# Strassen's scheme in the second layer of the second sweep too, in seven PSUM banks, with the tokens held once

## The chip, the cores and the metric

The kernel runs on one core of a Trainium2 chip. The metric is the time of one execution on the device, in microseconds (us); the median of three executions is given. Engines are TensorE (PE in the profile; PEld is its weight load), VectorE (DVE), ScalarE (ACT), GpSimd (POOL) and SyncE (SP), which issues the DMA transfers.

## The reference

Attention with a decay, then a mixing of the tokens and a two-layer perceptron with a residual. B = 8, H = 8, S = 576, D = 64, so d_model is 512; the hidden width is 2048, the rank of U V is 32. All is float32.

```python
def _attn_ref(q, k, v, f):
    scores = scale * np.matmul(q, k.transpose(0, 1, 3, 2))
    cum = np.cumsum(np.log(np.clip(f, 0.0001, 1.0)), axis=-1)
    scores = np.where(causal, -1000000000.0, scores + cum[:, :, :, None] - cum[:, :, None, :])
    ...                                   # softmax over the last axis
    return np.matmul(attn, v)

def _moe_ref(x, U, V, w_ch1, w_ch2):      # x: 8 x 576 x 512
    h = x.transpose(0, 2, 1) @ U @ V
    u = x + h.transpose(0, 2, 1)
    return u + np.maximum(u @ w_ch1, 0.0) @ w_ch2
```

## The kernel before

Every float32 operand of a product is held as a high and a low part in the matmul's own format, and a product is three matmuls: high by high, low by high, high by low. `split` makes the two parts: a cast on ACT (L182) and a subtraction on DVE or POOL (L185).

The hidden layer has 16 chunks of 128. A first sweep computes the attention batch by batch, the mixing, u, and the part of the perceptron of the first 6 chunks, and leaves u (`ud`, both parts) and the running output (`accd`) in DRAM. The second sweep, which the change touches, does the other NB = 10 chunks, whose weights (b1h, b1l, b2h, b2l) DVE and ACT decode into SBUF in its first part (L65 to L71). Tokens are worked on in nine groups of 512: the first 512 of each batch, and one group of the eight last 64.

Group 0 is plain: `first` (L979) and the plain second layer. Groups 1 to 8 take the chunks in five pairs (`pair_of_chunks`). The first layer of a pair is a product of 2 x 2 blocks by the scheme of Strassen and Winograd: seven products (m1 to m7) of six matmuls of 256 columns (`product`, L1069), each in one of two psF or two psX banks. DVE adds them up from PSUM (L1092; the copy of m1 to s1 is ACT's, L1100), and ACT and DVE make the relu and its split (L970, L971). The second layer (`second`, L993) is plain: per pair eight units of three matmuls of 512 columns, which add up over the ten chunks in four psO banks. `go` issues three, three and two of the units of the pair before between the products of a pair.

The scheme needs sums of blocks of the weights (`weight_sums`, DVE and ACT, made once at the start) and of the tokens. For these, POOL makes eight sums per group (`token_sums`, L1052 to L1057) in `whole_u`, which lies in xn[2], and in the last pair of a group, when each part has been read for the last time, `token_part` splits it into Th (ACT) and Tl (POOL). A group's u comes by two transfers of 1 MB (`load_u`, L962) into one of two buffers, its running output by one (L1138), and its four outputs are stored at the end (L999) after DVE's last adds (L997).

PE's order is the program's; the other engines' queues are ordered by a scheduler from a model of the kernel. On the chip each queue runs in the order it was given, and an instruction waits for semaphores. Waits on PSUM are by bank.

Of the kernel before, what the change touches and what calls it, by code (L numbers as in the profile page):

```python
# [40 lines left out]
def tile_decay_attention_moe(ctx, tc, qk, v, f, U, V, w1, w2, out):  # L41
# [917 lines left out]
    def load_u(g):  # L959
        t = up.tile([P, 2, NDC, MAIN], F32R, tag="u", name=f"u{g}")  # L960
        for x in range(2):
            nc.sync.dma_start(t.bitcast(F32)[:, x], ud[g, :, x])  # L962
# [22 lines left out]
    def second(z, i, h, x):

        k = z["done"][x]
        z["done"][x] += 1
        if k == 0:
            z["po"][x] = psO.tile([P, DM], F32, tag="O", name=f"O{z['g']}_{x}")  # L990
        po = z["po"][x]
        for m, (ht, wt_) in enumerate(((h[0], b2h), (h[1], b2h), (h[0], b2l))):
            nc.tensor.matmul(po, ht[:, P * x : P * x + P], wt_[i], start=k == 0 and m == 0, stop=k == NB - 1 and m == 2)  # L993
        if k < NB - 1:
            return
        g, o = z["g"], z["acc"][:, x]
        nc.vector.tensor_tensor(o, po, o, op=ALU.add)  # L997
        if g < B:
            nc.sync.dma_start(out[g, P * x : P * x + P], o)  # L999
# [9 lines left out]
    for i in range(NB // 2):  # L1009
# [35 lines left out]
    whole_u = xn[2][:, 0:4].rearrange("p q (c t) -> p q c t", c=2)  # L1045

    def token_sums(u):

        for q in range(4):
            c, t = 2 * (q // 2), HT * (q % 2)  # L1050
            h, l = (x[:, c : c + 2, t : t + HT].bitcast(F32) for x in u)
            nc.gpsimd.tensor_tensor(whole_u[:, q], h, l, op=ALU.add)  # L1052
# [6 lines left out]
    def token_part(q):  # L1059
        split(Th[:, q], Tl[:, q], whole_u[:, q], nc.scalar, nc.gpsimd)  # L1060
# [3 lines left out]
    def product(bank, tag, name, a, b):  # L1064
        ps = bank.tile([P, 512], F32, tag=tag, name=name)[:, 0:HT]
# [7 lines left out]
    def pair_of_chunks(z, u, i, ready, renew):  # L1073

        def go(k):
            for fn in ready[:k]:
                fn()
            del ready[:k]  # L1080
# [130 lines left out]
```

## Time and profile before

| | us |
|---|---|
| three executions | 1246.3, 1245.42, 1245.12; median 1245.42 |
| profiled execution | 1242.59, span 1240.8, granted TensorE clock 0.999 |
| PE, PEld busy | 1204.0, 1066.0 |
| DVE, ACT, POOL busy | 861.3, 645.5, 424.5 |
| second sweep, group 0 | about 753 to 806 |
| groups 1 to 8 | 806 to 1237; 52.8 a group from the second on (u loads at 860.43, 913.25, 966.08) |

In rows of a timeline stand: start, duration, engine, line, operation, output and input tiles with their shapes, how many, and in brackets the idle time of the engine before and what ended it. The chain's rows have start, duration, engine, tile, line and count. `SPq` is a DMA that SP issues.

### The profile page before, as it was taken

Reading aid. Unit: us, or ns where it says so; the run is one execution under the profiler, and the core shown is the slowest. Engines: PE = TensorE matmul, PEld = TensorE weight load, DVE = VectorE, ACT = ScalarE, POOL = GpSimd, SP = SyncE. Lnnn points to the kernel's source line nnn. Section 1 sums busy time; section 2 is a strip of 40 time slices with the busy share of each in tenths; the row PEclk is TensorE's granted clock in tenths of the full one; section 3 lists DMA queues with packets and bytes.
Section 4 is the critical chain, followed back from the end, with each engine's and each line's share of the span. In section 5 each row is a group of like instructions: output and inputs, shape, how many; then the busy total and the mean of one; then the engine's idle time right before and its main releaser. Section 6 shows DMA issues by size and latency. Waiting matters only on the chain.

```text
span 1240.8 us, 21851 instructions
## 1 busy us (share of the span) xinstructions
PE 1204.0 (97%) x7824; PEld 1066.0 (86%) x7824; DVE 861.3 (69%) x2195; ACT 645.5 (52%) x1741; POOL 424.5 (34%) x377
## 2 busy tenths in 40 slices
PE   8998999999999999999999999989999999999998
PEld 5776898998989988989989888878988889888897
DVE  8877778768778778787686799684554645546443
ACT  5777678767778758777675444322122221212211
POOL 4223454534544435454541000441341413315100
PEclk9999999999999999999999999999999999999999
DMA  6544344525335325425342345121120312213010
GB/s 183 153 132 130 79 105 111 151 68 159 95 89 164 88 78 148 117 71 171 79 125 76 120 141 229 34 69 69 68 102 35 136 43 95 85 52 137 1 35 35
DMA packets 67581, 125.87 MB, mean 101 GB/s; under 512 B 7408, under 2 KB 31984, under 8 KB 65424
## 3 DMA queue, kind: packets, MB, share of 16 engines
q1 hardware_dynamic: 67408, 124.47, 32.8%
q8 instruction: 62, 1.02, 0.3%
q14 instruction: 47, 0.39, 0.1%
q10 hardware_dynamic: 64, 0.00, 0.0%
HBM read 88.65 MB, written 35.78 MB: 100 GB/s over the span
## 4 chain that ended last, share of the span: by engine, by line
PE 82%; DVE 8%; ACT 6%; issue 2%; DMA 2%; SPq 0%; ACTq 0%; POOL 0%; DVEq 0%; POOLq 0%
PE O L993 20%; PE M L1069 16%; PE A L700 10%; PE B L718 9%; PE V L543 5%; PE T L440 3%; PE S L344 3%; PE Hb L979 2%; PE V L515 2%; PE S L345 2%; ACT P L373 1%; ACT G L309 1%; PE Tt L609 1%; PE St L344 1%; PE S L341 1%
## 5 line engine op out<-in xcount | busy, mean ns | idle before, releaser
L1092 DVE TENSOR_TENSOR sum<-M,sum 128x256 f32<-128x256 f32 x280 | 117.7, 422 | 173.3 <-PE M L1069 172.3
L970 ACT ACTIVATE bh<-sum 128x256 fp32r<-128x256 f32 x160 | 66.3, 418 | 256.9 <-DVE sum L1092 256.8
L373 ACT ACTIVATE P<-S,nm 128x128 f32<-128x128 f32 (+3 forms) x256 | 137.5, 539 | 57.5 <-DVE nm L365 48.3
L365 DVE CUSTOM_DVE_ANT_0 S<-S,mask 128x128 f32<-128x128 f32 (+3 forms) x256 | 125.7, 495 | 53.5 <-PE S L345 46.8
L993 PE MATMUL O<-b2h,bh 128*128 128x512 f32 x360 | 143.0, 397 | 0.0
L993 PE MATMUL O<-b2l,bh 128*128 128x512 f32 x360 | 142.4, 396 | 0.0
L993 PE MATMUL O<-b2h,bl 128*128 128x512 f32 x360 | 141.8, 394 | 0.0
L700 PE MATMUL A<-uh,w1h 128*128 128x256 f32 (+1 forms) x384 | 120.3, 313 | 1.8 <-DVE hl L704 1.7
L309 POOL CAST G<-qk 64x576 fp32r<-64x576 f32 x52 | 34.9, 671 | 250.1 <-PE St L345 149.5
L700 PE MATMUL A<-ul,w1h 128*128 128x256 f32 (+1 forms) x384 | 113.5, 296 | 0.0
L700 PE MATMUL A<-uh,w1l 128*128 128x256 f32 (+1 forms) x384 | 113.5, 296 | 0.0
L185 POOL TENSOR_TENSOR Tl<-xn,Th 128x512 fp32r<-128x512 f32 x32 | 41.3, 1303 | 201.7 <-PE M L1069 178.1
L971 DVE SCALAR_TENSOR_TENSOR bl<-sum,bh 128x256 fp32r<-128x256 f32 x160 | 92.4, 581 | 19.4 <-ACT bh L970 19.0
L1052 POOL TENSOR_TENSOR xn<-u 128x512 f32<-128x512 f32 x32 | 43.7, 1391 | 167.6 <-DVE b1l L71 106.4
L718 PE MATMUL B<-w2h,hh 128*128 128x512 f32 x216 | 90.4, 418 | 2.3 <-DVE hl L704 1.3
L440 PE MATMUL T<-ident,P 128*128 128x128 f32 x544 | 85.5, 273 | 0.0
L718 PE MATMUL B<-w2l,hh 128*128 128x512 f32 x216 | 85.1, 394 | 0.0
L718 PE MATMUL B<-w2h,hl 128*128 128x512 f32 x216 | 84.6, 392 | 0.0
L422 DVE TENSOR_TENSOR PTl<-T,PTh 128x512 fp32r<-128x512 f32 (+1 forms) x156 | 79.0, 524 | 6.6 <-ACT PTh L419 6.3
L993 PEld LDWEIGHTS O<-b2l,bh 128*128 128x128 f32 x360 | 67.7, 188 | 16.5
L322 POOL TENSOR_TENSOR G<-qk,G 64x576 fp32r<-64x576 f32 x52 | 74.4, 1431 | 15.6 <-ACT G L309 6.2
L993 PEld LDWEIGHTS O<-b2h,bl 128*128 128x128 f32 x360 | 68.2, 189 | 11.2
(240 smaller groups left out, 3543.7 us busy)
## 6 DMA issues: line engine op xcount, KB each, us to landing
qk<-in_qk_dram SPq DMA_DIRECT2D x104, 288.0 KB
u<-ud SPq DMA_DIRECT2D x16, 1024.0 KB
sr<-in_w_dram SPq DMA_DIRECT2D x20, 512.0 KB
vr<-in_v_dram SPq DMA_DIRECT2D x32, 256.0 KB
accd<-ost SPq DMA_DIRECT2D x32, 256.0 KB
xn<-accd SPq DMA_DIRECT2D x8, 1024.0 KB
out_dram<-xn SPq DMA_DIRECT2D x32, 256.0 KB
ud<-uh SPq DMA_DIRECT2D x7, 1024.0 KB
```

The lines of the kernel that those rows point to most:

```text
L322: pin(el.tensor_tensor(g[oth, 2, cols], k[oth], gf[oth, 2, cols], op=ALU.subtract))
L365: nc.vector.tensor_tensor_reduce(ps[:, :w], ps[:, :w], mask[:, 512 - w : 512], scale=-SCALE, scalar=3.0e38, op0=ALU.add, op1=ALU.min, accu ...
L373: nc.scalar.activation(pt, ps[:, :w], AF.Exp, bias=z["nm"][:, col : col + 1], scale=-1.0, accum_out=z["sm"][:, col : col + 1])
L422: defer(2, lambda: nc.vector.tensor_tensor(dstl, src, dsth.bitcast(F32), op=ALU.subtract))
L440: nc.tensor.transpose(tp[:, P * x : P * x + P], z["P"][j][i][:, P * c : P * c + P], ident)
L700: nc.tensor.matmul(ps[:, :nt], wt[:, fc, c], ut[:, c, sl], start=m == 0, stop=m == 3 * NDC - 1)
L718: nc.tensor.matmul(ps, ht[:, fc, P * x : P * x + P], wt[:, fc], start=fc == 0 and m == 0, stop=fc == NA - 1 and m == 2,)
L970: nc.scalar.activation(hh, src, AF.Relu)
L971: nc.vector.scalar_tensor_tensor(hl, src, 0.0, hh.bitcast(F32), op0=ALU.max, op1=ALU.subtract)
L993: nc.tensor.matmul(po, ht[:, P * x : P * x + P], wt_[i], start=k == 0 and m == 0, stop=k == NB - 1 and m == 2)
L1069: nc.tensor.matmul(ps, a[x][:, c], b[y][:, c], start=m == 0, stop=m == 5)
L1092: nc.vector.tensor_tensor(dst, ps, other, op=ALU.add)
```

## The change

The second layer of groups 1 to 8 goes by the same scheme. The hidden blocks X11, X12, X22 and four sums of them (S3, S1, S2, S4) lie in one buffer `hb`. After a pair's m3, DVE makes the four sums from relus with four instructions (L1218 to L1221), and ACT and POOL split them (L185). `output_products` then gives seven units of 2 x 3 matmuls of 256 columns (L1130), which add up over the five pairs of a group in seven banks, five of psM and two of psF. One such unit stands after each first-layer product. At the end of a group, in pair 0 of the next, the seven banks are combined into the four quadrants of the output: eight adds on DVE, a copy to u4 on ACT and three adds on POOL (all in `ends`, by `add`, L1112); only then are the quadrants stored.

All first-layer products use the two halves of one bank, `halves`. Tokens are held once: three blocks that enter a product as they are come into `direct` (six transfers of 256 KB, L969, in the last pair of the group before), and `load_whole` (L973) brings the high parts into xn[2] and the low ones into xn[0], from which POOL makes the token sums in place (L1086 to L1091). `acc` has one home, xn[1] (load L1265).

`weight_sums2` makes the sums of blocks of w2 on POOL and ACT: twelve POOL instructions of 128x256 for each of five pairs, four pairs in group 0 and the last in group 1.

```diff
-    up = pool("up", 2)
-    hp_ = pool("hp", 4)
-    psO = ctx.enter_context(tc.tile_pool(name="psO", bufs=4, space=PSUM, reuse_waits="tile"))
-    psX = ctx.enter_context(tc.tile_pool(name="psX", bufs=2, space=PSUM, reuse_waits="tile"))
+    psM = ctx.enter_context(tc.tile_pool(name="psM", bufs=1, space=PSUM, reuse_waits="tile"))
+    psL = ctx.enter_context(tc.tile_pool(name="psL", bufs=1, space=PSUM, reuse_waits="tile"))
+    direct = two.tile([P, 3, 2, 2, HT], F32R, name="direct")
+    hb = two.tile([P, 7, 2, HT], F32R, name="hb")
+    def load_direct(g, k):
+        c, t = ((0, 0), (2, 0), (2, HT))[k]
         for x in range(2):
+            nc.sync.dma_start(direct.bitcast(F32)[:, k, x], ud[g, :, x, c : c + 2, t : t + HT])
+    def load_whole(g):
+        for x, home in enumerate((xn[2], xn[0])):
+            nc.sync.dma_start(home[:, 0:NM], ud[g, :, x])
...
+    wides = [sf2.tile([P, 2 * HT], F32, tag="ost", name=f"sum{x}") for x in range(2)]
+    ends = sf.tile([P, 2 * HT], F32, tag="TS", name="sum2")
+    tmp = [t[:, HT * y : HT * y + HT] for t in [ends] + [x[:, NM] for x in xn] for y in range(2)]
+    def weight_sums2(i):
+        eng = nc.gpsimd
+        def whole(dst, r, c):
+            h, l = block2(i, r, c)
+            eng.tensor_tensor(dst, h.bitcast(F32), l.bitcast(F32), op=ALU.add)
...
+        for src, (h, l) in zip((t1, t0, t2, t3), [block2(i, 0, 1)] + SD[i]):
+            split(h, l, src, nc.scalar, eng)
+    halves = psL.tile([P, 2, HT], F32, name="halves")
+    def product(a, b):
+        ps = halves[:, turn[0] % 2]
+        turn[0] += 1
...
+    def output_products(z, i):
+        def ends_1():
+            nc.scalar.copy(u4, z["M"][1])
+            add(quarter[0], z["M"][1], quarter[0])
+        def ends_6():
+            add(u4, z["M"][6], u4)
+            add(u3, z["M"][7], u4)
+            add(u4, z["M"][5], u4)
+            for q in (2, 3):
+                add(quarter[q], u3, quarter[q], nc.gpsimd)
...
+        def ends_3():
+            add(quarter[1], z["M"][3], quarter[1])
+            add(quarter[1], u4, quarter[1], nc.gpsimd)
...
+        work = (
+            (1, X11, block2(i, 0, 0)), (4, X22, sd[2]), (2, X12, block2(i, 1, 0)), (7, S3, sd[0]),
+            (5, S1, block2(i, 0, 1)), (6, S2, sd[1]), (3, S4, block2(i, 1, 1)),
+        )
...
+        m1 = pr(1, block(i, 0, 0), D1)
         nc.scalar.copy(s1, m1)
+        slot(1)
+        m6 = pr(6, W2, T2)
+        add(s2, m6, s1)
+        slot(6)
+        m5 = pr(5, W1, T1)
+        add(s4, m5, s2)
+        slot(5)
+        m2 = pr(2, block(i, 0, 1), D2)
+        add(c11, m2, s1)
+        relu(*X11, c11)
+        slot(2)
+        m7 = pr(7, W3, T3)
+        add(c22, m7, s4)
+        add(s2, m7, s2)
+        relu(*X22, c22)
+        slot(7)
+        m4 = pr(4, block(i, 1, 1), T4)
+        add(c21, m4, s2)
+        relu(*X12, c21)
+        slot(4)
+        m3 = pr(3, W4, D3)
+        add(c12, m3, s4)
+        slot(3)
+        nc.scalar.activation(r21, c12, AF.Relu)
+        nc.vector.scalar_tensor_tensor(c22, c22, 0.0, r21, op0=ALU.max, op1=ALU.add)
+        nc.vector.scalar_tensor_tensor(r21, c11, 0.0, r21, op0=ALU.max, op1=ALU.subtract)
+        nc.vector.scalar_tensor_tensor(c11, c11, 0.0, c22, op0=ALU.max, op1=ALU.subtract)
+        nc.vector.scalar_tensor_tensor(c21, c21, 0.0, c11, op0=ALU.max, op1=ALU.add)
+        for src, (h, l) in ((r21, S3), (c22, S1), (c11, S2), (c21, S4)):
+            split(h, l, src, nc.scalar, nc.gpsimd)
+        ready.extend(output_products(z, i))
...
+                def renew(k):
+                    if k in (1, 2, 3):
+                        load_direct(nxt, k - 1)
+                    else:
+                        token_part({6: 3, 5: 0, 7: 1, 4: 2}[k])
+                pair_of_chunks(z, i, ready, renew if nxt is not None and i == NK - 1 else None, 1 if n > 1 or i else 2)
...
+                if i == 1:
+                    nc.sync.dma_start(xn[1][:, 0:NM], accd[g].rearrange("x p d -> p x d"))
+                    if nxt is not None:
+                        load_whole(nxt)
+                if i == 2 and nxt is not None:
+                    token_sums()
```

**How it moves instructions.** First PE, inside a pair. Before (m3, then the last two units of the second layer, then the next pair's first product; M are first-layer products, O second-layer sums, sw block sums of weights):

```order
L1069 MATMUL M_6_2_13911<-u_13136,swhh 128x256 [waits DVE_49]
L1069 MATMUL M_6_2_13911<-u_13136,swhl 128x256
...
L993 MATMUL O_2_13775<-b2h_9166,bh_2_13739 128x512
L993 MATMUL O_2_13775<-b2h_9166,bl_2_13740 128x512
L993 MATMUL O_2_13775<-b2l_9176,bh_2_13739 128x512
L993 MATMUL O_3_13800<-b2h_9166,bh_2_13739 128x512
...
L1069 MATMUL M_6_3_13933<-u_13136,b1h_9150 128x256 [waits DVE_49]
```

And after (from the unit of S2 past m5's follower to m2 and m7; halves is the one bank of the first layer, N the banks of the second):

```order
L1130 MATMUL N_8_13974<-b2h_9173,hb 128x256 x2
L1130 MATMUL N_8_13974<-b2l_9183,hb 128x256
...
L1107 MATMUL halves<-direct,b1h_9144 128x256 [waits DMAHW7_49,DVE_49]
L1107 MATMUL halves<-direct,b1l_9154 128x256
...
L1130 MATMUL N_8_13990<-sw_9772,hb 128x256 [waits Activation_49]
L1130 MATMUL N_8_13990<-sw_9772,hb 128x256 [waits Pool_49]
L1130 MATMUL N_8_13990<-sw_9772,hb 128x256 x4
L1107 MATMUL halves<-Th,swhh 128x256 [waits DVE_49]
```

Units of the second layer and products now alternate one by one; every product waits for the reader of the one before it, since both lie in one bank, and the units of S sums wait for POOL's splits.

Second POOL, from the end of one of the groups to the second pair of the next. Before:

```order
L1055 TENSOR_TENSOR xn_107<-xn_107 128x512
L1056 TENSOR_TENSOR xn_107<-xn_107 128x512
L1057 TENSOR_TENSOR xn_107<-xn_107 128x512
L185 TENSOR_TENSOR Tl<-xn_107,Th 128x512 x4
L1052 TENSOR_TENSOR xn_107<-u_13136 128x512 x4
```

After (xn_107 is xn[2], xn_105 is xn[0], xn_106 is xn[1] with `acc`; sum_9780 and sum_9781 are u3 and u4; hb rows are the splits, in the order S3, S1, S2, S4):

```order
L185 TENSOR_TENSOR Tl<-xn_107,Th 128x512 x3
...
L1086 TENSOR_TENSOR xn_107<-xn_107,xn_105 128x2x256 x4
L1088 TENSOR_TENSOR xn_107<-xn_107 128x2x256
L1089 TENSOR_TENSOR xn_107<-xn_107 128x2x256
L1090 TENSOR_TENSOR xn_107<-xn_107 128x2x256
L1112 TENSOR_TENSOR xn_106<-sum_9780,xn_106 128x2x256 x2
L1091 TENSOR_TENSOR xn_107<-xn_107 128x2x256
L185 TENSOR_TENSOR hb<-xn_106,hb 128x256
L1112 TENSOR_TENSOR xn_106<-sum_9781,xn_106 128x2x256
L185 TENSOR_TENSOR hb<-xn_106,hb 128x256
L185 TENSOR_TENSOR hb<-xn_105,hb 128x256
```

Between the Tl rows and the sums stand the four splits of pair 4, left out here; the three hb rows at the end are S3, S1 and S2 of the new group's pair 0, so they stand behind seven and eight token sums.

Third DVE, in pair 1 of a group. Before (the sums s2, s4, c11 and s3 of pair 1, then a relu's split; sum tiles are the temporaries):

```order
L1092 TENSOR_TENSOR sum_9780<-M_6_1_13751,sum_9780 128x256 [waits PE_49,Activation_49]
L1092 TENSOR_TENSOR sum_9781<-M_6_1_13759,sum_9780 128x256 [waits DVE_49,PE_49]
L1092 TENSOR_TENSOR sum_9782<-M_6_1_13779,sum_9780 128x256 [waits PE_49]
L1092 TENSOR_TENSOR sum_9781<-M_6_1_13787,sum_9780 128x256 [waits PE_49]
L971 SCALAR_TENSOR_TENSOR bl_2_13740<-sum_9782,bh_2_13739 128x256 [waits Activation_49]
```

After (the third row is c11 = m2 + s1 of pair 1):

```order
L1221 SCALAR_TENSOR_TENSOR sum_9782<-sum_9782,xn_105 128x256 [waits DVE_49]
L1112 TENSOR_TENSOR xn_105<-halves,xn_107 128x256 [waits PE_49]
L1112 TENSOR_TENSOR xn_105<-halves,sum_9782 128x256 [waits DVE_49,PE_49,Pool_49]
L977 SCALAR_TENSOR_TENSOR hb<-xn_105,hb 128x256 [waits Activation_49]
L1112 TENSOR_TENSOR xn_106<-halves,xn_105 128x256 [waits PE_49]
```

The add of c11 has a wait for POOL, which is the split of S2 of the pair before, from the same buffer.

More of the change, by code (lines that the diff above doesn't have):

```diff
@@ L980, in first, with store @@
                 m += 1
-        h = hidden(f"{g}_{i}")
-        relu(h, ps, slice(0, MAIN))
-        return h
[L985 to L997, printed above, removed]
+        flat = hb.rearrange("p k x t -> p (k x t)")[:, 2 * MAIN * (i % 3) : 2 * MAIN * (i % 3) + 2 * MAIN]
+        h = flat[:, 0:MAIN], flat[:, MAIN : 2 * MAIN]
+        relu(*h, ps)
+        return h
+    def store(g, acc, x):
+        o = acc[:, x]
         if g < B:
@@ L1002, in second @@
             nc.sync.dma_start(out[2 * x, MAIN:S], o[64:128])
+    def second(z, i, h, x):
+        if i == 0:
+            z["po"][x] = psM.tile([P, DM], F32, tag=BANKS[x], name=f"O{z['g']}_{x}")
+        po = z["po"][x]
+        for m, (ht, wt_) in enumerate(((h[0], b2h), (h[1], b2h), (h[0], b2l))):
+            nc.tensor.matmul(po, ht[:, P * x : P * x + P], wt_[i], start=i == 0 and m == 0, stop=i == NB - 1 and m == 2)
+        if i < NB - 1:
+            return
+        o = z["acc"][:, x]
+        nc.vector.tensor_tensor(o, po, o, op=ALU.add)
+        store(z["g"], z["acc"], x)
     n3 = 3 * 2 * P
@@ L1008, in tile_decay_attention_moe @@
     SW = []
-    for i in range(NB // 2):
+    for i in range(NK):
         blocks = []
@@ L1059, in token_part @@
     def token_part(q):
-        split(Th[:, q], Tl[:, q], whole_u[:, q], nc.scalar, nc.gpsimd)
+        split(Th[:, q], Tl[:, q], whole_u[q], nc.scalar, nc.gpsimd)
     T1, T3, T4, T2 = ([x[:, q] for x in (Th, Tl)] for q in range(4))
-    def product(bank, tag, name, a, b):
-        ps = bank.tile([P, 512], F32, tag=tag, name=name)[:, 0:HT]
+    halves = psL.tile([P, 2, HT], F32, name="halves")
+    turn = [0]
+    def product(a, b):
+        ps = halves[:, turn[0] % 2]
+        turn[0] += 1
         m = 0
@@ new lines, in pair_of_chunks, with pr, slot @@
+    def pair_of_chunks(z, i, ready, after, each):
+        g = z["g"]
+        W1, (W2, W3, W4) = block(i, 1, 0), SW[i]
+        D1, D2, D3 = ([direct[:, k, x] for x in range(2)] for k in range(3))
+        s1, s2, s4, c11, c22, r21 = tmp[0:6]
+        if i % 2:
+            s2 = tmp[6]
+        c21, c12 = s2, s4
+        def pr(k, a, b):
+            return product(a, b)
+        def slot(k):
+            for fn in ready[:each]:
+                fn()
+            del ready[:each]
+            if after:
+                after(k)
+        m1 = pr(1, block(i, 0, 0), D1)
+        nc.scalar.copy(s1, m1)
+        slot(1)
[29 more added lines that the diff above has]
+        ready.extend(output_products(z, i))
@@ new lines, in tile_decay_attention_moe @@
+        z = {"g": order[0], "acc": xn[1], "po": [None] * NM}
+        load_whole(order[1])
+        for k in range(3):
+            load_direct(order[1], k)
+        for i in range(NB):
+            h = first(order[0], cur, i)
+            for fn in ready:
+                fn()
+            ready = [lambda z=z, x=x, i=i, h=h: second(z, i, h, x) for x in range(NM)]
+            if i % 2 and i < 6:
+                weight_sums(i // 2)
+            if i % 2 and i > 2:
+                weight_sums2((i - 3) // 2)
+            if i == NB - 4:
+                token_sums()
```

167 lines of the change are left out of this document (74 added, 93 removed).

## The prediction

> **What bounds the kernel now.** I read the page first: its busy shares and the chain that ended last.
>
> ```profile
> PE 1204.0 (97%) x7824; PEld 1066.0 (86%) x7824; DVE 861.3 (69%) x2195; ACT 645.5 (52%) x1741; POOL 424.5 (34%) x377
> PE 82%; DVE 8%; ACT 6%; issue 2%; DMA 2%; SPq 0%; ACTq 0%; POOL 0%; DVEq 0%; POOLq 0%
> PE O L993 20%; PE M L1069 16%; PE A L700 10%; PE B L718 9%; PE V L543 5%; PE T L440 3%; PE S L344 3%; PE Hb L979 2%; PE V L515 2%; PE S L345 2%; ACT P L373 1%; ACT G L309 1%; PE Tt L609 1%; PE St L344 1%; PE S L341 1%
> ```
>
> TensorE is the bound, and 36% of the span are the two lines that the change touches. An average says little of one stage, so I took busy time by stretches (PE, PEld, DVE, ACT, POOL, then clock, DMA share, GB/s).
>
> ```profile
> 757.00:808.00 51.00, 51.00 (x228) 41.40 (x227) 40.29 (x82) 18.83 (x37) 15.04 (x12) 1.00 0.28 105
> 808.00:820.00 12.00, 8.56 (x55) 7.61 (x54) 12.00 (x29) 3.45 (x9) 2.67 (x2) 0.95 0.27 91
> 873.00:926.00 53.00, 53.00 (x334) 47.62 (x333) 27.74 (x62) 12.56 (x30) 16.86 (x14) 1.00 0.22 80
> ```
>
> From group 2 on (873 to 926) PE never pauses and the others are half idle. Group 0 (to 808) is PE-bound with DVE at 40 of 51 us; the start of group 1 waits for DVE. Last I read the chain in order of time for one pair of chunks.
>
> ```profile
> 830.05 2.13 PE M L1069 x18
> 832.18 2.10 PE O L993 x9
> 834.29 1.42 PE M L1069 x12
> 835.71 2.09 PE O L993 x9
> 837.80 1.43 PE M L1069 x12
> ...
> 840.61 2.12 PE M L1069 x18
> ```
>
> A pair takes 840.61 - 830.05 = 10.56 us. A matmul of 256 columns costs 2.13/18 = 0.1185 us, one of 512 columns 2.10/9 = 0.2335 us.
>
> **Term 1, the gain.** A pair's second layer is 24 matmuls of 512 columns, 24 x 0.2335 = 5.60 us; it becomes 42 of 256, 42 x 0.1185 = 4.98 us. Eight groups of five pairs: 40 x 0.62 = **-24.8 us**. It is certain, since these matmuls are back to back now and the order puts them on the same engine. Everything else is waits.
>
> **Term 2, one bank for the first layer.** Product k+1 now waits for whoever reads product k, with one slot of six second-layer matmuls between (6 x 0.1185 = 0.71 us). The hand-over is seen here:
>
> ```profile
> 1226.35 0.28 PE L1069 MATMUL M<-Tl,sw 128*128 128x256 f32 x1
> 1226.66 0.42 DVE L1092 TENSOR_TENSOR sum<-M,sum 128x256 f32<-128x256 f32 x1 [0.28 <-PE M L1069]
> 813.67 0.41 DVE L1092 TENSOR_TENSOR sum<-M,sum 128x256 f32<-128x256 f32 x1
> 814.13 0.39 PE L1069 MATMUL M<-u,swhh 128*128 128x256 f32 x1 [0.85 <-DVE sum L1092]
> ```
>
> A product's last matmul starts 0.31 us before DVE's add, the add takes 0.42, and PE goes on 0.05 after its end: 0.78. PE comes to the next product 0.12 + 0.71 = 0.83 after that start, so one reader is hidden by the slot. Product 7 has two readers (c22 and s2), the second a further 0.34: 0.3 us late, once a pair, 40 x 0.3 = **+12 us**. Below: nothing, were the two adds of product 7 free by chance; above 0.7 a pair, where a DVE instruction with a longer wait stands ahead.
>
> **Term 3, POOL between two groups (n = 2 to 7).** This decides. The queue of POOL has, after the splits of pair 4, the next group's token sums, two quadrant adds, and only then S3, S1 and S2 of pair 0, with a sum and another add among them. The single buffer c11 makes the add of product 2 in pair 1 wait for the split of S2, and product 7 behind it waits for that add. What POOL's instructions cost, and when its data come:
>
> ```profile
> 614.75 0.46 POOL L594 TENSOR_TENSOR xh<-xn,xh 64x128 fp32r<-64x128 f32 x1
> 615.29 1.29 POOL L595 TENSOR_TENSOR xl<-xn,xh 128x512 fp32r<-128x512 f32 x1
> 869.05 5.42 POOL L1052 TENSOR_TENSOR xn<-u 128x512 f32<-128x512 f32 x4 [7.42 <-DMA u<-ud]
> 874.43 1.47 POOL L1054 TENSOR_TENSOR xn<-xn 128x512 f32<-128x512 f32 x1
> 877.35 1.30 POOL L1056 TENSOR_TENSOR xn<-xn 128x512 f32<-128x512 f32 x1
> 913.15 1.31 POOL L185 TENSOR_TENSOR Tl<-xn,Th 128x512 fp32r<-128x512 f32 x1 [1.40 <-ACT Th L182]
> 913.25 0.80 SPq L962 DMA_DIRECT2D u<-ud  x2
> 921.13 5.43 POOL L1052 TENSOR_TENSOR xn<-u 128x512 f32<-128x512 f32 x4 [6.67 <-DMA u<-ud]
> ```
>
> Call T the end of a group's last first-layer product (913.2 here: the loads of 2 MB go out with it). The last Tl ends 913.15 + 1.31, T + 1.3, and the load of the high part now waits for just that. 2 MB took 921.13 - 913.25 = 7.9 us; now it is 1 MB with 0.5 MB of direct blocks ahead, between 3.9 and 7.9, by bytes 5.9: POOL starts its sums at T + 7.2. Seven sums took 877.35 + 1.30 - 869.05 = 9.6 us. A 128x256 instruction isn't in the rows: 0.46 us at 128 elements and 1.29 at 512 put it at 0.74, with a gap 0.82; an add of a quadrant has 512, so 1.37. Two adds, the eighth sum, S3, an add, S1, S2: 4 x 1.37 + 3 x 0.82 = 7.9. S2 is done at T + 24.7, product 7 of pair 1 can start at T + 25.2. Undelayed it starts 23 blocks of six matmuls after T, at 23 x 0.711 = T + 16.4. So PE waits 8.8 us a group, first (about 6.5) for S3, then for S2; I take **6 x 9 = +54 us**, 7 to 12 a group by the load's bounds and by DVE below. Before, the same sums stood ahead of nothing: the next POOL work that PE needs was 26 us away.
>
> Such a wait has a second price, seen once before:
>
> ```profile
> 818.41 0.38 PE L1069 MATMUL M<-Th,swhh 128*128 128x256 f32 x1 [2.59 <-DVE sum L1092]
> 819.51 0.41 PE L1069 MATMUL M<-Th,b1h 128*128 128x256 f32 x1
> 822.07 0.48 PE L993 MATMUL O<-b2h,bh 128*128 128x512 f32 x1
> ```
>
> After 2.59 us of idleness the matmuls stand 0.213 us apart until 822.07 and the granted clock of that stretch is 0.95: 3.2 us at half speed, 1.4 us lost. Once a group: **+8 us** (0 to 2.8 each). [...]
>
> **Term 4, groups 8 and 1.** Group 8 has no token sums: two adds of POOL ahead of S3, one more before S1. Only the s2 add (the split of S4 before it) and the c11 add wait, some 2.5 and 2 us: **+4.5**. Group 1 has the token sums spread by weight sums that still occupy DVE: **+4** (2 to 8).
>
> **Term 5, the start of the sweep.** The plain group 0 hides DVE's decoding of the weights at present. POOL now adds some 44 instructions of 0.8 us there for second-layer sums. What a POOL instruction does to DVE:
>
> ```profile
> 822.29 0.42 DVE L1092 TENSOR_TENSOR sum<-M,sum 128x256 f32<-128x256 f32 x1
> 822.51 1.29 POOL L1052 TENSOR_TENSOR xn<-u 128x512 f32<-128x512 f32 x1 [11.85 <-DVE sw L185]
> 822.62 1.46 DVE L1039 TENSOR_TENSOR xn<-xn 128x256 f32<-128x256 f32 x1
> 793.74 1.28 DVE L71 TENSOR_TENSOR b2l<-xn,b2h 128x512 fp32r<-128x512 f32 x2
> 794.50 2.92 POOL L1052 TENSOR_TENSOR xn<-u 128x512 f32<-128x512 f32 x2 [5.37 <-DVE b2l L71]
> 803.99 3.81 POOL L185 TENSOR_TENSOR Tl<-xn,Th 128x512 fp32r<-128x512 f32 x3 [1.20 <-ACT Th L182]
> 806.23 2.13 PE M L1069 x18
> ```
>
> DVE's SBUF-to-SBUF add took 1.46 us under a POOL add, 0.42 when alone; one that reads PSUM wasn't held. So decoding, done at 795.0 now, ends later: by nothing at the least, by 25 us if all 44 are paid for, and I take 8. The high tokens then load into the decoder's scratch, 5 us; POOL's sums, rest of the weight sums and splits up to T2 are ten of 1.37 and eight of 0.82, 20 us. Product 6 of group 1, which started at 806.9, starts at 795 + 8 + 5 + 20 = 828, 21 later, less some 3 of the DVE waits of 808 to 820 that fall into it: **+18** (4 to 36).
>
> **Term 6, the end.** Now:
>
> ```profile
> 1230.15 7.02 PE O L993 x30
> 1235.09 2.79 DVE L997 TENSOR_TENSOR xn<-O,xn 128x512 f32<-128x512 f32 x4 [3.57 <-PE O L993]
> 1235.81 2.43 SPq L999 DMA_DIRECT2D out_dram<-xn  x4
> ```
>
> The last pair's products now need four more DVE steps, casts and splits, and behind them stand u3, u4, POOL adds and then the stores: **+5** (3 to 7).
>
> Sum: -24.8 + 12 + 54 + 8 + 8.5 + 18 + 5 = +80.7. The profiled run took 1242.59 us for a span of 1240.8; the median of the runs shown is 2.8 higher, 1245.4, which gives **1326 us**. With the low ends (0, 42, 0, 5, 4, 3) it is 1275, with the high ends (28, 72, 17, 14, 36, 7) 1395; not all fall one way, so 1288 to 1362 is this case's own range.
>
> **Rivals.** (a) POOL comes in time and each reader hides behind its slot: the gain stands alone, less the end: 1245.4 - 24.8 + 5 = 1226 us, faster. For it: POOL is busy 16.9 of 53 us now, and with 20 splits of 0.82 and three adds of 1.37 more still under 40, so capacity is there. It decides where S2 of pair 0 is split by T + 16: the load would have to land at T - 1.5, before its own buffer is free. (b) The sums on POOL don't hold PE but banks, start and end do: terms 1, 2, 4, 5 and 6, 1264 us; were the start hidden too, 1246, no change. For it speaks only that the sums' order follows from a program and could be overtaken, but a queue isn't overtaken. (c) DVE becomes the bound in the whole sweep: seven of its instructions a pair have both inputs in SBUF, and POOL is busy most of the time; at 0.4 to 1 us each, as in the row of 822.62, that is 3 to 7 us, and DVE's 27.7 of 53 us with some 6 more leave a pair a slack of 3; some 2 us more in 30 pairs: 1326 + 60 = 1386 us. [...] Against (c): splits come four in a pair and are short, 3.3 of 10 us.
>
> **How the numbers follow.** Forecast 0.66; (a) 0.10; (b) 0.13, of which 0.03 lie by no change and 0.02 below; (c) 0.11. A measurement of this kernel tells about 0.2%, 2.5 us, from no change. Faster 0.12, same 0.03, slower 0.85. The range 1238 to 1372 leaves out (a), most of (c) and little of the forecast's ends, some 2 in 10. The likeliest case has 1288 to 1362.
>
> **What would show it.** Right: a group period of 61 to 63 us where it was 52.8, with PE idle once or twice a group in the slot of product 7 of pair 1, released by hb from POOL and by the c11 add; POOL's sums directly before, waiting for DMA; m4 waiting 0.3 us a pair; a slow clock for some 3 us in each group; PE idle 10 to 25 us after group 0. Wrong: groups of 50 to 52 us with PE at 95% and more (a, b), or PE idle in all pairs behind DVE with long L977 and L1218 to L1221 (c).

## The result, and the profile after

The changed kernel takes 1366.89 us (median of four executions, 1362.78 to 1371.32) against 1245.27 us before: a ratio of 1.0977, 95% interval 1.0941 to 1.1012 (the 1245.27 is the median with a fourth execution). The profiled execution has a span of 1364.6 us at a granted clock of 0.977; before it was 1240.8 us.

From the page after, busy shares and the chain that ended last by engine:

```profile
PE 1244.7 (91%) x8544; PEld 1118.5 (82%) x8544; DVE 985.3 (72%) x2347; ACT 715.4 (52%) x1929; POOL 635.2 (47%) x621
PE 54%; DVE 20%; POOL 8%; ACT 7%; issue 6%; DMA 4%; SPq 0%; POOLq 0%; ACTq 0%; DVEq 0%
```

PE's share of the chain fell from 82% to 54%. No engine became full: what took its place are hand-overs between engines. By stretches (PE, PEld, DVE, ACT, POOL, clock, DMA share, GB/s), the start of the sweep, a middle stretch, and inside it one pair that nothing disturbs:

```profile
757.00:808.00 51.00, 40.54 (x155) 30.50 (x154) 47.98 (x75) 19.47 (x42) 39.46 (x37) 0.93 0.24 79
808.00:850.00 42.00, 26.90 (x112) 21.13 (x110) 25.38 (x43) 10.96 (x24) 28.62 (x29) 0.84 0.23 78
1090.00:1150.00 60.00, 53.20 (x388) 50.34 (x387) 37.54 (x73) 17.21 (x43) 31.42 (x32) 0.94 0.26 88
1130.30:1141.40 11.10, 10.88 (x84) 10.36 (x84) 6.31 (x14) 3.39 (x10) 2.99 (x5) 1.00 0.01 2
```

The last row has a trap: PE looks busy in 10.88 of 11.10 us, but its 84 matmuls need 84 x 0.1185 = 9.95 us back to back. Each matmul's record is longer than its place in the pipeline (0.28 us against 0.1185), so short waits vanish in the busy share. They show in the starts.

From the starts of the first-layer products in PE's timeline, the sweep divides so (us; group 1 from the old start of its first product, 806.06, to the first product of group 2):

| | before | after | difference |
|---|---|---|---|
| start and group 1, to | 861.60 | 903.99 | +42.4 |
| groups 2 to 7, each | 52.83 | 64.17 | +11.35, six: +68.1 |
| group 8, to its last product | 51.3 | 59.9 | +8.6 |
| from there to the end | 10.9 | 15.7 | +4.8 |

Together +123.9 us, the difference of the spans. A group of 64.2 us is five pairs: some 14.9 (pair 0) and 15.2 (pair 1), then 11.1, 11.1 and 11.8.

An undisturbed pair, from the chain in order of time:

```profile
1130.32 0.98 PE halves L1107 x6
1131.30 0.72 PE N L1130 x6
1132.02 0.78 PE halves L1107 x6
1132.80 0.72 PE N L1130 x6
1133.52 0.86 PE halves L1107 x6
...
1134.40 0.42 DVE xn L1112
1134.83 0.34 DVE sum L1112
...
1135.21 0.98 PE halves L1107 x6
...
1138.70 0.44 DVE xn L1218
...
1140.71 0.26 issue
1140.97 0.42 DVE xn L1112
1141.39 0.04 issue
1141.43 0.97 PE halves L1107 x6
```

A pair takes 1141.43 - 1130.32 = 11.11 us. Between m7 and m4 stand the two adds that read m7 (1134.40 to 1135.17); before the next m5 (1141.43) stands the add of s2, which in DVE's queue comes behind the four sums that begin at 1138.70.

The boundary of two groups, from the chain (the DMA row, the load of the next tokens) and the timelines of POOL, DVE and PE (its first row is m3 of the group's last pair):

```profile
1094.57 0.96 PE L1107 MATMUL halves<-direct,sw 128*128 128x256 f32 x6
1096.36 7.27 DMA xn<-ud
...
1098.41 2.29 POOL L185 TENSOR_TENSOR hb<-xn,hb 128x256 fp32r<-128x256 f32 x3 [2.50 <-ACT hb L182]
1100.67 0.71 POOL L185 TENSOR_TENSOR hb<-sum,hb 128x256 fp32r<-128x256 f32 x1
1101.42 0.42 DVE L1112 TENSOR_TENSOR sum<-halves,sum 128x256 f32<-128x256 f32 x1 [0.79 <-POOL hb L185]
1101.90 0.39 PE L1107 MATMUL halves<-Th,b1h 128*128 128x256 f32 x1 [2.18 <-DVE sum L1112]
1103.79 5.19 POOL L1086 TENSOR_TENSOR xn<-xn,xn 128x512 f32<-128x512 f32 x4 [2.40 <-DMA xn<-ud]
1112.28 1.36 DVE L1218 SCALAR_TENSOR_TENSOR xn<-xn 128x256 f32<-128x256 f32 x1
1113.31 2.89 POOL L1112 TENSOR_TENSOR xn<-sum,xn 128x512 f32<-128x512 f32 x2
1115.45 0.38 PE L1107 MATMUL halves<-Th,b1h 128*128 128x256 f32 x1 [1.10 <-DVE xn L1112]
1117.58 0.91 POOL L185 TENSOR_TENSOR hb<-xn,hb 128x256 fp32r<-128x256 f32 x1
1118.29 0.38 PE L1107 MATMUL halves<-direct,b1h 128*128 128x256 f32 x1 [1.16 <-DVE xn L1112]
1119.68 1.41 POOL L185 TENSOR_TENSOR hb<-xn,hb 128x256 fp32r<-128x256 f32 x2
1120.46 1.44 PE L1130 MATMUL N<-sw,hb 128*128 128x256 f32 x5 [1.07 <-POOL hb L185]
1121.12 0.42 DVE L1112 TENSOR_TENSOR xn<-halves,sum 128x256 f32<-128x256 f32 x1 [2.88 <-POOL hb L185]
1121.69 0.49 PE L1107 MATMUL halves<-Th,swhh 128*128 128x256 f32 x1
```

Two of PE's stops here come from a split on POOL that a single buffer waits for: m5 of pair 0 (1101.90), whose forerunner s2 waits for the split of S4 of the pair before (POOL, 1100.67), and m7 of pair 1 (1121.69), behind the c11 add that waits for S2 (POOL, 1119.68). From 1103.79 on POOL works without a gap through token sums, adds and splits. Between these two stops PE also waits 1.10 us at m5 (1115.45) and 1.16 us at m2 (1118.29) of pair 1, behind adds in DVE's queue: DVE's four sums (L1218 to L1221) take 0.90 to 1.38 us each there, beside POOL; in the undisturbed pair three take 0.42 to 0.43 us, and the last, beside a split on POOL, 0.97. And the unit of S3 (1120.46) waits 1.07 us for POOL.

And the start, from the timelines of DVE and POOL and the chain (its `xn<-ud` row is the load of the tokens):

```profile
815.96 0.69 DVE L71 TENSOR_TENSOR b2l<-xn,b2h 128x512 fp32r<-128x512 f32 x1
816.67 5.00 DMA xn<-ud
821.81 5.02 POOL xn L1086 x4
836.55 0.58 PE L1107 MATMUL halves<-Th,swhh 128*128 128x256 f32 x1 [8.30 <-ACT Th L182]
851.71 4.93 DMA xn<-ud
856.79 5.51 POOL xn L1086 x4
```

Decoding ends at 816.65 us, where it ended at 795.0 before; m6 of group 1 starts at 836.55 instead of 806.8. Then the next group's tokens, which come into the scratch that the first layer's weight sums use until 851.6, arrive at 856.6, and POOL's first splits in group 1 stand behind their sums.

### The profile page after: what moved, and what is told of

The parts are those of the page before. It is cut to its first block, busy times and chain, and to the rows that moved or that the text cites. A ratio compares the mean times of both kernels' runs of the same rounds, so it can differ in the third digit from the quotient of the medians.

```text
span 1364.6 us, 24372 instructions
## 1 busy us (share of the span) xinstructions
PE 1244.7 (91%) x8544; PEld 1118.5 (82%) x8544; DVE 985.3 (72%) x2347; ACT 715.4 (52%) x1929; POOL 635.2 (47%) x621
## 4 chain that ended last, share of the span: by engine, by line
PE 54%; DVE 20%; POOL 8%; ACT 7%; issue 6%; DMA 4%; SPq 0%; POOLq 0%; ACTq 0%; DVEq 0%
PE halves L1107 10%; PE A L700 9%; PE B L718 9%; PE N L1130 5%; PE V L543 5%; PE T L440 3%; DMA xn<-ud 3%; DVE xn L1112 3%; POOL xn L1086 3%; PE V L515 2%; PE S L344 2%; PE S L345 2%; POOL hb L185 2%; DVE sum L1112 1%; ACT G L309 1%
## 5 line engine op out<-in xcount | busy, mean ns | idle before, releaser
L185 POOL TENSOR_TENSOR hb<-xn,hb 128x256 fp32r<-128x256 f32 x136 | 103.6, 786 | 203.5 <-ACT hb L182 203.5
L976 ACT ACTIVATE hb<-xn 128x256 fp32r<-128x256 f32 x96 | 40.0, 417 | 190.1 <-DVE xn L1112 190.1
L1130 PE MATMUL N<-b2h,hb 128*128 128x256 f32 x640 | 124.3, 286 | 0.0
L1130 PE MATMUL N<-sw,hb 128*128 128x256 f32 x624 | 95.6, 288 | 7.6 <-POOL hb L185 7.6
L1130 PEld LDWEIGHTS N<-b2h,hb 128*128 128x128 f32 x640 | 100.8, 193 | 0.1
L1130 PEld LDWEIGHTS N<-sw,hb 128*128 128x128 f32 x624 | 84.5, 195 | 9.3 <-POOL hb L185 9.3
L1130 PE MATMUL N<-b2l,hb 128*128 128x256 f32 x320 | 91.3, 285 | 0.0
L1107 PE MATMUL halves<-direct,b1h 128*128 128x256 f32 x320 | 78.4, 307 | 12.6 <-DVE xn L1112 12.6
L1112 DVE TENSOR_TENSOR xn<-halves,sum 128x256 f32<-128x256 f32 x80 | 33.7, 422 | 76.1 <-PE halves L1107 56.5
L1107 PE MATMUL halves<-Th,b1h 128*128 128x256 f32 x160 | 54.2, 339 | 34.2 <-DVE sum L1112 19.8
L322 POOL TENSOR_TENSOR G<-qk,G 64x576 fp32r<-64x576 f32 x52 | 74.4, 1432 | 15.6 <-ACT G L309 6.2
```

Of the source, the lines that this page charges most:

```text
L185: leng.tensor_tensor(dl, src, dh.bitcast(F32), op=ALU.subtract)
L322: pin(el.tensor_tensor(g[oth, 2, cols], k[oth], gf[oth, 2, cols], op=ALU.subtract))
L1107: nc.tensor.matmul(ps, a[x][:, c], b[y][:, c], start=m == 0, stop=m == 5)
L1112: eng.tensor_tensor(dst, a, b, op=ALU.add)
L1130: nc.tensor.matmul(ps[:, y], a[p_][:, P * y : P * y + P], w[q_], start=i == 0 and y == 0 and m == 0, stop=i == NK - 1 and y == 1 and m == 2,)
```

## The experiments

**POOL's queue.** PE's order is the program's by `manual_schedule`; the edit puts POOL under it too, and moves the token sums into the middle of a group.

```diff
+    with tc.manual_schedule(engines={ET.PE, ET.Pool}):
         for n in range(1, NG):
...
-                if i == 2 and nxt is not None:
-                    token_sums()
+                if i == 1 and nxt is not None:
+                    token_wholes()
+                if i == 2 and nxt is not None:
+                    token_sums(False)
```

> From group 1 on POOL's queue has the program's order, and the next group's token sums stand in the middle of a group: four behind the splits of pair 1, four behind those of pair 2. Nothing else is changed. Theory A (the token sums ahead of S3, S1 and S2 of pair 0 are what holds TensorE at the start of a group): pair 1 of groups 2 to 7 falls from 13.8 to 17.3 us to about 11.1, pair 0 keeps only the 2.1 us for the split of S4, so a group falls from 63.6 to about 58 us, six groups give 35 us, the whole about 1330 us. Rival B (the waits at the boundary are DVE's, which has the eight group-end adds there, and POOL is merely busy): pair 0 and pair 1 stay within 1 us, the whole above 1355 us. Rival C (the sums in the middle of a group hold the splits of pairs 2 and 3 instead): pairs 0 and 1 fall as in A, pairs 3 and 4 grow by the same, no change in sum.

It took 1346.53 us, 20 less than the changed kernel. Of the 22.8 us between the two spans 16.3 are groups 2 to 7; 4.4 are an earlier start of group 2 (899.6 us), with POOL's order in group 1 changed too. The edit moved one more thing, the first product of group 1, which begins at 758.6 us inside group 0 (0.7 us of work). Pair 1 is 12.7 us and the same in all groups, pair 0 is 13.4, but pairs 2 and 3 grew to 11.4 and 11.6: a group is 61.5 us. So the token sums ahead of the splits cost 30.1 - 26.1 = 4.0 us a group in pairs 0 and 1, not 8.8 (group 8 of the changed kernel, which has no token sums, takes 14.7 + 12.7 there, 2.7 less than the others). A is right in kind, but said twice the size; 0.8 us of the gain goes again in pairs 2 and 3, which is rival C's way in small. In their place this stop is left, from the timelines of POOL, DVE and PE:

```profile
1026.34 0.71 POOL L185 TENSOR_TENSOR hb<-sum,hb 128x256 fp32r<-128x256 f32 x1
1027.09 0.42 DVE L1116 TENSOR_TENSOR sum<-halves,sum 128x256 f32<-128x256 f32 x1 [1.12 <-POOL hb L185]
1027.57 0.39 PE L1111 MATMUL halves<-Th,b1h 128*128 128x256 f32 x1 [2.33 <-DVE sum L1116]
```

It is the wait of s2 for S4, which no token sum causes.

**Products in twos.** m1 and m6 are issued together, then two units, then m5 and m2, and so on; the adds follow each two.

```diff
         m1 = pr(1, block(i, 0, 0), D1)
+        m6 = pr(6, W2, T2)
         nc.scalar.copy(s1, m1)
-        slot(1)
-        m6 = pr(6, W2, T2)
         add(s2, m6, s1)
+        slot(1)
         slot(6)
```

> First-layer products are issued two at a time into the two halves of the one bank, then two units of the second layer: DVE reads both while 1.42 us of units run. The same matmuls, adds and splits. Theory A (an ordinary pair takes 11.11 instead of 9.95 us because each product must wait for the reader of the one before, seven hand-overs a pair): four hand-overs a pair are left, with 1.42 us to hide them; a pair takes 10.0 to 10.5 us, and 40 pairs give 25 to 40 us, less what the boundary takes back, the whole 1330 to 1345 us. Rival B (the 1.16 us a pair are the chain from m3 over the relu and four DVE sums to the next s2): a pair stays at 10.9 us and more, the whole above 1355 us.

1351.18 us. An ordinary pair takes 10.45 us, inside A's range, so four hand-overs in place of seven give back 0.66 of the 1.16 us. The whole gained 16 instead of 25 us and more: a group fell by 1.8 us only, since pairs 0 and 1 together take 30 us as before: the faster pairs reach the same POOL stop earlier and wait longer there.

**Both.** The first two edits in one kernel.

> The first two edits together. If the two terms are separate (POOL's queue at the boundary, the hand-over inside a pair), their gains add: about 35 + 30 us, the whole 1295 to 1310 us, a group of 2 to 7 at 53 to 54 us. If they hide one another (a faster pair reaches the next wait sooner), the whole stays above 1315 us.

1340.07 us, so they hide one another: 27 us where 20 and 16 would add to 36. A group is 61.2 us, hardly less than with POOL's order alone; pair 0 grew to 15.0 us, and pairs 2 and 3, beside which the token sums now run, take 11.1 us where group 8, which has none, takes 10.2.

**The buffer of s2.** One line: its parity runs over all pairs instead of within a group.

```diff
-        if i % 2:
+        if (z["n"] * NK + i) % 2:
             s2 = tmp[6]
```

> The changed kernel with one line different: the buffer of s2 alternates through all pairs; there, five pairs being odd, pair 4 of a group and pair 0 of the next use the same one, and the first add of the group waits for POOL's split of S4. Theory A (in groups 2 to 7 POOL's queue sets the time, and this wait only comes before the same stop): pair 0 becomes 2.1 us shorter and pair 1 as much longer, no change in groups 2 to 7; group 8, without token sums, gains 2.1 us; the whole 1362 to 1367 us. Rival B (each wait at the boundary adds to the time by itself): 2.1 us less in each of seven groups, the whole about 1352 us.

1355.3 us, 11.6 less, near rival B: pair 0 fell to some 12.2 us (and to 11.3 in group 8), pair 1 stayed between 14.4 and 17.3. But the one line also changed POOL's queue, which the scheduler orders anew: in the timeline two of the eight token sums now stand behind S2 (L1090 and L1091, at 1053.67 and 1055.04, after the splits at 1051.62). So this run doesn't tell A from B in groups 2 to 7. The next one does, since there POOL's order is fixed:

> POOL in program order, products in twos, and s2's buffer alternating. With POOL's queue out of the way the wait for S4 stands alone: pair 0 falls from 15.0 to 12.9 us or less in groups 2 to 8, 15 us in all, the whole about 1325 us. If DVE, with eight group-end adds in pair 0, is the true limit there, pair 0 stays above 14 us and the whole above 1335 us.

1310.64 us, 29 less than without the line. Pair 0 fell from 15.0 to 10.9 us in each group, twice the 2.1 us of the wait. Most of the rest is the clock, by an estimate from the mean granted clocks: 1337.6 x (1 - 0.974) = 34.8 us were lost with the wait, 1310.8 x (1 - 0.983) = 22.3 are now, 12.5 less. A group takes 57.1 us, still 4.3 more than before, and this is the fastest of the variants: 5.35% slower than the kernel before (4.78 to 5.91%).

**No token sums.** The first experiment's kernel without the eight sums in groups 2 to 8.

> As the first experiment (POOL in program order), with the token sums of groups 2 to 8 left out; their transfers and splits stay. Theory A (POOL's 1.4 us instructions also hold DVE's instructions with both inputs in SBUF, wherever they stand): pairs 2 and 3 fall from 11.5 to 11.1 us or less and a group from 61.3 to about 60 us, pairs 0 and 1 stay at 13.4 and 12.7; the whole about 1338 us. Rival B (the token sums no longer cost anything in the middle of a group): no change, 1346 us.

1343.40 us. Pairs 2 and 3 fell to 10.9 us, 0.5 to 0.7 less each, more than A said; but pair 0 rose from 13.4 to 14.8, and a group stays at 61.1 us. The mean granted clock was 0.972 against 0.983, and matmuls that come soon after the stop for S4 are longer in the mean (m2 among `halves<-direct,b1h`, 314 ns against 304, and the S units, `N<-sw,hb`, 290 against 283); that the rise of pair 0 is the clock's is an estimate from these means. The sums do cost time in the middle of a group; the total shows it only in part.

**One bank or two.** Product 5 of the second layer adds into the bank of product 6, and its bank goes to the first layer, so that products alternate between banks.

```diff
-    halves = psL.tile([P, 2, HT], F32, name="halves")
+    two_banks = [psL.tile([P, 512], F32, name="halves"), psM.tile([P, 512], F32, tag="M5", name="halves2")]
...
-        ps = halves[:, turn[0] % 2]
+        ps = two_banks[turn[0] % 2][:, 0:HT]
...
+            if i == 0 and k == 6:
+                z["M"][6] = z["M"][5]
```

> The changed kernel with the first layer in two banks instead of one. The second bank is that of product 5 of the second layer, which here adds into the bank of product 6 (so the quadrants get another sum; as many matmuls, adds and stores). Theory A (the hand-over of the one bank costs the 1.16 us of an ordinary pair): each product then follows with no wait for the reader of the one just before, and a pair takes 9.95 to 10.2 us, 0.9 to 1.1 us less in each of some 24 undisturbed pairs, about 25 us, the whole about 1340 us. Rival B (the order of DVE's queue, the four sums ahead of the next s2, costs them): a pair stays at 10.8 us or more, the whole above 1355 us.

1337.07 us, and an ordinary pair of 9.96 us: all of the 1.16 us is gone, the part behind the four sums too. The chain in order of time, and the same stretch by engines:

```profile
1120.92 0.72 PE halves L1107 x6
1121.64 0.72 PE N L1132 x6
1122.36 0.71 PE halves L1107 x6
1123.06 0.71 PE N L1132 x6
...
1112.00:1142.00 30.00, 30.00 (x255) 30.00 (x255) 18.91 (x42) 12.67 (x31) 13.89 (x16) 1.00 0.11 37
```

No wait is left in such a pair; with all seven accumulators, however, it would be nine banks, one more than the eight of the changed kernel (five of psM, two of psF, one of psL). The whole fell by 30 us, a little more than A's 25, but by another account: in groups 2 to 7 pairs 2 to 4 gave 4.1 us a group and pair 0 another 2.9 (12.0 instead of 14.9), and pair 1 took 4.3 of it back. It takes 19.1 to 19.8 us, a group 61.4, since the stop for POOL doesn't move when the pairs get shorter. It now stands whole at the unit of S3:

```profile
1104.83 1.43 PE L1132 MATMUL N<-sw,hb 128*128 128x256 f32 x5 [5.72 <-POOL hb L185]
```

That pair 0 fell shows that a part of the stop for S4 came through the scarce bank too: m5 no longer waits for the s2 add, and m2 waits 1.7 us instead.

**Second-layer weight sums.** First left out:

```diff
-        t0, t1, t2, t3 = (w[:, HT * y : HT * y + HT] for w in wides for y in range(2))
...
+        return
...
-        sd = SD[i]
+        sd = [block2(i, 0, 0), block2(i, 1, 0), block2(i, 1, 1)]
```

> The sums of blocks of the second layer's weights are left out (no weight_sums2 on POOL and ACT); the units that need them multiply by plain blocks instead, as many matmuls of the same shapes. Theory A (the 44 POOL instructions in group 0 lock DVE out while it decodes the weights, and their rest stands ahead of the token sums): decoding ends near 796 instead of 816.7 us, m6 of group 1 starts near 810 instead of 836.6 us, and the start of group 2 falls from 904 to about 877 us: 27 us less, the whole about 1340 us. Rival B (the delay comes from the tokens, which now load into the decoder's scratch and so wait for the last decode): m6 of group 1 starts no earlier than 795 + 5 + 14 = 814 us and group 1 still takes 70 us and more, the whole above 1350 us.

1345.79 us, 21 less; m6 of group 1 starts at 815.9 us (822.8, which the next expectation takes for it, is m5) and group 2 at 884.5 us, 19.5 earlier. From DVE's timeline, the last decode:

```profile
799.08 0.68 DVE L71 TENSOR_TENSOR b2l<-xn,b2h 128x512 fp32r<-128x512 f32 x1
```

It ends 17 us earlier. The whole lies between A and B: the sums cost 19.5 us, not 27, and m6 still waits for the tokens and starts after B's 814 us. The next kernel takes that away too, by lending the tokens and the first layer's weight sums the space of `sw2`:

```diff
-        load_whole(order[1])
+        load_whole(order[1], first_hi)
...
-                    spare = xn[2].rearrange("p c d -> p (c d)")
+                    spare = sw2.bitcast(F32)[:, 2048 : 2048 + 1280]
```

> As the third experiment (no sums of second-layer weights), and the space that this frees takes the high tokens of group 1 and the scratch of the first layer's weight sums in group 1, so neither the first tokens nor those of group 2 wait for a scratch. Theory A (of the 42 us that the start lost, 20 are the weight sums on POOL and the rest the tokens' waiting for scratch): m6 of group 1 starts at 807 to 812 us instead of 822.8, group 2 at about 868 instead of 884.5; the whole about 1329 us. Rival B (the rest is group 1's own DVE work, the weight sums of pairs 3 and 4 and the group's end): group 2 starts at 880 us or later, the whole above 1341 us.

1333.55 us, nearer to A; group 2 starts at 873.0. m6 of group 1 starts at 817.1, later than in the kernel before it, but behind the last units of group 0 and without a wait; the gain lies in pairs 0 and 1 of group 1 (6.9 and 4.5 us). So of the 42.4 us at the start 19.5 are the second-layer weight sums, 11.5 the scratch, and 11.4 are left, of which 2.8 are the pairs' own difference (five times 11.11 - 10.56). Then a kernel that does the whole work, with the sums of pairs 1 to 4 in group 1 (in the kernel of three edits):

```diff
-            if i % 2 and i > 2:
-                weight_sums2((i - 3) // 2)
+            if i == 3:
+                weight_sums2(0)
...
-                if n == 1 and i == 0:
-                    weight_sums2(NK - 1)
+                if n == 1 and i < NK - 1:
+                    weight_sums2(i + 1)
```

> The kernel of the sixth experiment with the sums of second-layer weights moved: pair 0's in group 0, those of pairs 1 to 4 into group 1, each one pair ahead of its use. Theory A (they cost the start of the sweep because they stand beside DVE's decoding): decoding ends near 800 us, m6 of group 1 starts near 820, group 1 becomes bound by POOL (9.4 us of sums and 3.3 of splits in a pair of 10 to 11, token sums besides) and takes 60 to 68 us, group 2 starts at 878 to 888 instead of 899.8 us; the whole 1290 to 1300 us. Rival B (POOL can't hold this pace and the units wait for their weights): group 1 takes over 80 us and the whole is 1310 us or more.

1315.36 us, 5 more than without the move, which is rival B's time (its 80 us for group 1 are not quite reached: 77.8 from m6 to group 2). Pair 1 of group 1 starts 15.6 us earlier (836.8 instead of 852.4), and of that 3.3 are left when group 2 starts (896.6 instead of 899.8): pairs 3 and 4 of group 1 take 19.0 and 17.8 us, and pair 0 of group 2 takes 17.4 instead of 10.9. From 820 to 897 us PE waits 8.6 us for POOL (weight sums and splits) and 10.2 us for DVE; how much of the second is POOL's doing was not separated.

**Token sums on DVE.** In the kernel of three edits:

> The kernel of the sixth experiment with the eight token sums of a group on DVE instead of POOL. Theory A (POOL's long instructions lock DVE out, and this is why pairs 2 and 3 take 11.1 us where group 8, without sums, has 10.2): DVE pays 8 x 0.6 = 4.8 us of its own time in a group, in which it is idle for a third, pairs 2 and 3 fall to 10.5 us and the whole to 1300 us or less. Rival B (DVE's queue is what PE waits for in every pair, so 4.8 us more on it cost as much as the lock): no change, 1306 to 1316 us.

1337.98 us, 27 more, outside both. Pairs 2 and 3 take 10.2 us, as A said. The scheduler put all eight sums on DVE ahead of the add of m3 in pair 0, which became 16.6 to 18.0 us long. From the waits of PE over groups 2 to 7 (engine, line waited for, us in total, times, longest), here and in the kernel of three edits:

```profile
PE halves L1111 <- DVE xn L1116: 42.8, 22, 5.3
```

```profile
PE halves L1111 <- DVE xn L1116: 23.8, 36, 0.9
```

The last kernel therefore fixes DVE's order as well and spreads the sums over pair 2:

> The kernel of the sixth experiment with the token sums on DVE again, but from group 1 on DVE's queue too has the program's order, and the sums stand one or two after each product's adds in pair 2 of a group, so that no add of a product stands behind all eight. Theory A (POOL's sums lock DVE out, and the tenth experiment lost its gain only because they all stood ahead of the add of m3 in pair 0): pair 2 takes 10.4 to 11 us, pair 3 10.2, and a group 55.5 to 56.3 instead of 57.1 us; the whole 1300 to 1306 us. Rival B (DVE's own time is the limit): pair 2 takes 12 us or more and the whole stays at 1309 us or above. Neither theory puts it below the kernel before, since the start (38 us) and the boundary stay.

1343.23 us (ratio 1.0776, 1.0752 to 1.0799). Pair 3 takes 10.2 us, as A said; pair 2 takes 11.6, more than with the sums on POOL (11.1), between the two theories; the total is B's. What decided the total is neither: with DVE in program order, three group-end adds stand ahead of m3's add, so that pair 0 takes 12.7 instead of 10.9 us, and the first layer's weight sums stand in one piece in group 1, so that group 2 starts at 915.1 instead of 899.8 us. So that POOL's sums cost the pairs beside them 0.9 us each is shown; that they would be cheaper elsewhere is not.

## Why the prediction was right, and where it was not

It said slower, 1326 us, range 1238 to 1372; measured 1367 us, 41 above the forecast (43 in the spans). That is inside the range, but 5 us from its upper end and outside the 1288 to 1362 that the forecast called its own; that the range held owes something to luck. Two terms were much too small, by 34 and 18 us, and one was too large by 9, which kept the sum inside. With the spans' +123.9 us shared out by the starts above:

| term | forecast | measured | from |
|---|---|---|---|
| 1, fewer columns | -24.8 | -24 | two banks: 9.96 instead of 10.56 us a pair, x 40 |
| 2, one bank | +12 | +46 | 11.11 - 9.95 = 1.16 a pair, x 40 |
| 3 and 4, boundaries of groups 2 to 8, with the clock | +66.5 | +57 | 68.1 + 8.6, less 35 pairs of terms 1 and 2 (+19.3) |
| 5 and group 1's part of 4 | +22 | +40 | 42.4, less five pairs of terms 1 and 2 (+2.8) |
| 6, the end | +5 | +4.8 | last product to the end |

Terms 1 and 2 are measured in undisturbed pairs and carried over to all 40; the third and fourth row are what is left after that. In the pairs at a boundary a hand-over can hide in a longer wait, so the line between terms 2 and 3 is not sharp.

**Term 1** held: matmuls of 256 columns stand 0.1185 us apart after as before.

**Term 2** failed in the sentence "one reader is hidden by the slot". The margin that it had left there, 0.05 us, was too thin. Measured, the starts of two products stand 1.49 to 1.54 us apart at an ordinary hand-over instead of 1.42, and the first matmul of a product takes 0.18 to 0.23 us to the next instead of 0.12 (1133.39 to 1133.61 in PE's timeline). m4 comes 0.40 late instead of 0.3, and m5 0.28 late for a reason that the working didn't have: the s2 add stands in DVE's queue behind the four sums that close the pair before. With two banks all of it goes, which makes the scarce bank the cause.

**Term 3** was right in its place and nearly in its time, wrong in what the token sums ahead of the splits were worth. T, the end of the group's last first-layer product, is 1095.5 here. POOL's queue went as forecast: seven sums in 9.6 us, and 7.7 instead of 7.9 from there to the end of S2. The load took 7.3 us where 5.9 was taken, within its bounds. So product 7 of pair 1, forecast for T + 25.2, starts at 1121.69, T + 26.2, behind exactly the c11 add and the split of S2 that were named; with two banks it is T + 26.0, though PE comes to that pair earlier. But the 9.8 us over T + 16.4 are not one wait. Where 6.5 us at S3 were forecast, 1.07 are seen (5.72 with two banks). PE had stood before at m5 of pair 0 (2.2 us, for S4) with a stretch of half clock behind it, and at m5 and m2 of pair 1 behind DVE. So taking the token sums out of the way gave 4.0 us a group, and the s2 buffer another 4.1 with its clock. The forecast counted the wait for S4 only for group 8. Pair 1 stays at 12.3 to 12.7 us where no token sum stands ahead; there DVE's group-end adds and POOL's three adds run side by side, and which of them holds it was not separated.

**The clock** was about right: one stretch a group, 8 us in all, was forecast. In groups 2 to 7 there are five stretches of 3.4 us at a granted clock of 0.50, from 929.1, 1038.3, 1103.2, 1120.3 and 1168.0 us: at most half of their 17 us, less where PE waits anyway. They don't fall one to a group: two lie in the group from 1096.6, none in two others.

**Term 5** was the right mechanism and half the size. Decoding ended 21.6 us later (8 was taken, 25 was the bound); without POOL's sums it ends 16.9 us earlier than that. DVE and POOL side by side, from their timelines:

```profile
770.90 0.80 POOL L1066 TENSOR_TENSOR sum<-b2h,b2l 128x256 f32<-128x256 f32 x1
771.02 0.96 DVE L65 TENSOR_SCALAR sr<-sr 128x512 int32<-128x512 int32 x1
773.66 1.23 DVE L71 TENSOR_TENSOR b1l<-xn,b1h 128x512 fp32r<-128x512 f32 x1
786.52 0.41 DVE L65 TENSOR_SCALAR sr<-sr 128x512 int32<-128x512 int32 x1
```

In this stretch, with POOL at work, DVE's instructions take some 0.55 us more than at 786 to 789 us, L65 too (0.96 against 0.41), though it has one input; why, the runs don't show. The forecast counted only instructions with two inputs. What it also left out is the second half of group 1: the next tokens' load into the first layer's scratch, which kept POOL, and with it the splits of pair 0, until 862 us.

**Of the rivals**, (a) and (b) are out: groups of 64 us, not 50 or 52.8. (c), DVE as the bound of the whole sweep, is out as stated (DVE is busy for 6.3 of the 11.1 us of a pair), though what it rests on, POOL holding DVE, costs 0.9 us in each pair that has token sums beside it and has a part, not measured alone, in PE's two stops behind DVE in pair 1 (0.9 to 1.1 and 0.6 to 1.2 us). The hand-over of the bank, the term that was furthest out, stood in none of them at more than its 12 us.

## What to carry to other kernels

Count the banks before the matmuls: seven accumulators left one of the kernel's eight, each product then waited for the reader of the one before, and 1.16 us of hand-over a pair was twice the 0.6 us that the cheaper scheme saves. The hand-over that was hidden by 0.05 us on paper was not hidden: its products stand 1.49 to 1.54 us apart instead of 1.42, with 0.06 to 0.11 us of it between a product's first two matmuls. And when several waits stand at one boundary, taking away one shows the next: two edits that won 20 and 16 us alone won 27 together, and one line that won 12 us alone won 29 on top of them.

## What the runs showed of the hardware

The granted TensorE clock fell to half after short pauses: PE had waited 2.18 us ahead of 1101.90, the clock was 1.00 from 1099.8 to 1103.1 and 0.50 from 1103.2 to 1106.6, and there the matmuls stood 0.21 us apart:

```profile
1103.60 0.41 PE L1107 MATMUL halves<-direct,b1h 128*128 128x256 f32 x1
1103.82 0.41 PE L1107 MATMUL halves<-direct,b1l 128*128 128x256 f32 x1
```

PE had not been idle all the time before the fall: it was busy for 1.20 of the 3.3 us from 1099.8 on. The fall didn't always come: of the seven waits of 2.18 to 2.20 us at m5 of pair 0, in groups 2 to 8, four were followed by a stretch of half clock and three were not. So two waits of equal length differed by up to 1.7 us, an estimate: half of a stretch of 3.4 us at 0.50. That alone doesn't explain why a group's time in the changed kernel varies from 63.6 to 65.3 us: two groups of 63.6 us have none and one.

Beside each other not only DVE's instructions were longer (the 0.96 against 0.41 us of L65), but POOL's too. From 784.6 to 793 us DVE's instructions stand back to back at their usual 0.40 to 0.68 us, and one POOL instruction, whose like takes 0.73 us at 819.00, took 5.96:

```profile
786.32 5.96 POOL L1066 TENSOR_TENSOR sum<-b2h,b2l 128x256 f32<-128x256 f32 x1
```

Which of the two gives way, and when, these runs don't show.
